# First token tiles on one DMA queue, the ScalarE table load ahead of its DMAs, and the up weights in a 3 + 4 split

## The chip, the core and the metric

The kernel runs on one core of a Trainium2 chip. The core has TensorE (matrix products, results in PSUM), VectorE (DVE), ScalarE (ACT), GpSimd (POOL) and SyncE (SP, which here only issues DMAs). DMAs are issued from the queues of SP and ScalarE and carried by 16 DMA engines. The metric is the device time of one execution in microseconds (us), the median of several runs; lower is better.

## The reference

The input x has 2048 tokens of width 448, in bf16. It is normalised per token (mean and variance, no scale), and the result goes into two branches whose outputs are added to x:

```
xn  = layernorm(x)
q, k, v = split(xn @ wqkv)            # 16 heads of 28
p   = softmax(q k^T * 28**-0.5)       # key j seen by query i if 0 <= i - j < 256
out = x + (p v) @ wo + (gelu(xn @ w_gate) * (xn @ w_up)) @ w_down     # inner width 1792
```

## The kernel before

Tokens are handled in 16 tiles of 128 and in four blocks of 512 queries. The program is written out in one order by hand. Each engine runs its own instructions in that order and waits on semaphores for the others, so an instruction that waits also holds up those behind it on its engine or queue.

**The start.** DMAs bring in the first token tiles (line 85: tile 0 on SP's queue; line 86: tile 1 on ScalarE's; line 87: tiles 2 and 3 on SP's). ScalarE then issues the first quarter of the query and of the key weights (line 89, into wraw), while SP issues the value weights (line 90), the weights of the last 64 input channels (lines 92 and 94), tiles 4 to 7 (line 95), the remaining query and key weights (line 97) and the up weights of five of seven pairs (line 98, through load_ffn, line 82, two DMAs, one for each half of the partitions). Each DMA takes the next of eight completion semaphores in turn, whichever queue it is issued from, and one that takes a semaphore a second time waits first for the earlier DMA to land. So SP can wait at line 97 for the DMAs that ScalarE issued at line 89.

Meanwhile DVE fills constants: eps, the zeros that TensorE's warm-up products read (line 124; the buffer is that of wo, whose weights arrive much later), the padding columns of the packed weights (lines 131 to 133), and masks, all ones at line 134, from which GpSimd later cuts triangles. At line 135 ScalarE loads the function table with ln and exp, which rstd needs.

TensorE runs nine warm-up products (line 150). For each of tiles 0 to 3 then follow: statistics on DVE (lines 155 and 156), the inverse deviation on ScalarE (160, 161), the normalisation on DVE (170), five transposes on TensorE (184, 186), and the copy of the transposed tile to xnT (187). A tenth warm-up product stands between the transposes of tiles 0 and 1. v_dense (line 191 through mm3) computes values, proj the first four heads' queries and keys, and qk_halves (197) adds the last 64 channels. DVE copies the keys to kT (245), and the scores (652), the exp (656) and the products with v (624) follow.

**Swapped copies.** The 448 input channels are 3.5 times 128. Work on 64-row halves runs two products side by side, one on each half of TensorE's rows, which needs x and some weights also with their halves exchanged. xsw is that copy of xnT, made by SP DMAs (swap, line 437); wvs (line 771) holds swapped value weights and wsq (line 443) swapped query and key weights. Tiles 4 and later are transposed by a DMA on SP's queue (line 176) instead of on TensorE.

**The first block.** In the plan of block 0 TensorE alternates between scores, the remaining projections and gen_up, which computes the up product of pairs of 128-column groups ahead of the gate (line 456, tiles ue). It does so for pairs 1, 2, 3, 0 and 4 in that order; for pairs 3 and 4 one of the two copies out of PSUM (line 473) is ScalarE's. Each pair reads its own columns of wu. Then come value, query and key products of the next block (lines 320 and 334), which read xsw, wvs and wsq, and then the gated part, which reads the gate weights wg and, for pairs 5 and 6, the rest of wu.

SP's order around the change: line 98's up weights, w3k (130), swap of block 0 (437), tiles 8 to 11 (740), the DMA transpose of tile 4 (176), wvs (771), the transposes of tiles 5 to 7, swap of block 1, wsq (443), the gate weights, the up weights of pairs 5 and 6 (line 788), tiles 12 to 15 (789), wo (793 and 794) and the down weights (797).

Of the kernel before, what the change touches and what calls it, by code (L numbers as in the profile page):

```python
# [13 lines left out]
f32 = mybir.dt.float32  # L14
i32 = mybir.dt.int32

S, D, H, Dh, F = 2048, 448, 16, 28, 1792
# [3 lines left out]
QB, NB = 512, 4  # L21
# [6 lines left out]
def kernel(  # L28
# [11 lines left out]
    nc = tc.nc  # L40
# [18 lines left out]
    xv = A_x.rearrange("b (n p) d -> p (b n) d", p=P)  # L59
# [3 lines left out]
    x_sb = const.tile([P, NT, D], bf16, name="x_sb")  # L63
# [4 lines left out]
    wu = const.tile([P, 7, F // 2], bf16, name="wu")  # L68
# [6 lines left out]
    def load_ffn(dst, w, pairs):  # L75

        wv64 = w.rearrange("(c p) (h n) -> p c h n", p=64, h=2)
        ns = slice(pairs.start * P, pairs.stop * P)  # L80
        for hi in range(2):
            nc.sync.dma_start(out=dst[64 * hi:64 * hi + 64, :, ns], in_=wv64[:, :, hi, ns])

    wqk = rows(A_wqkv, 0, 3)[:, :, 0:2 * D]
    nc.sync.dma_start(out=x_sb[:, 0, :], in_=xv[:, 0, :])
    nc.scalar.dma_start(out=x_sb[:, 1, :], in_=xv[:, 1, :])
    nc.sync.dma_start(out=x_sb[:, 2:4, :], in_=xv[:, 2:4, :])
    for c in (0, D):
        nc.scalar.dma_start(out=wraw[:, 0:3, c:c + 4 * Dh], in_=wqk[:, :, c:c + 4 * Dh])
    nc.sync.dma_start(out=wv[:, 0:3, :], in_=rows(A_wqkv, 0, 3)[:, :, 2 * D:3 * D])  # L90
# [4 lines left out]
    nc.sync.dma_start(out=x_sb[:, 4:8, :], in_=xv[:, 4:8, :])  # L95
    for c in (0, D):
        nc.sync.dma_start(out=wraw[:, 0:3, c + 4 * Dh:c + D], in_=wqk[:, :, c + 4 * Dh:c + D])
    load_ffn(wu, B_w_up, slice(0, 5))

    ident = const.tile([P, P], bf16, name="ident")  # L100
    make_identity(nc, ident[:, :])
# [6 lines left out]
    masks = const.tile([P, 3, 4, 64], bf16, name="masks")  # L108
# [11 lines left out]
    eps_t = const.tile([P, 1], f32, name="eps_t")  # L120
    nc.vector.memset(eps_t[:, :], 1e-5)
    warm = wo[:, :, :].rearrange("p g n -> p (g n)")
    for c in (slice(0, QB), slice(QB, 4 * D)):
        nc.vector.memset(warm[:, c], 0.0)
    wqp = const.tile([P, 3, H, 32], bf16, name="wqp")
    wkp = const.tile([P, 3, H, 32], bf16, name="wkp")
    w3p = const.tile([P, H, 32], bf16, name="w3p")
# [3 lines left out]
    nc.vector.memset(wqp[:, :, :, Dh:32], 0.0)  # L131
    nc.vector.memset(wkp[:, :, :, Dh:32], 0.0)
    nc.vector.memset(w3p[:, :, Dh:32], 0.0)
    nc.vector.memset(masks[:, :, :, :], 1.0)
    nc.scalar.preload_act_table_set("natural_log_exp_and_others")

    xnT = const.tile([P, 4, S], bf16, name="xnT")
    xsw = const.tile([P, 3, 2 * QB], bf16, name="xsw")
# [65 lines left out]
    def take(name, cols=QB, tag=None):  # L204

        tag = tag or spare[0]
        spare.remove(tag)  # L210
        ps = psum.tile([P, QB], f32, name=name, tag=tag, bufs=1)[:, 0:cols]
        held[id(ps)] = tag, ps
        return ps
# [46 lines left out]
    def gen_qk(gs, others):  # L260

        for g in gs:
            pq = take("pq")
            proj(pq, wqp, 0, g)
            yield 650
            pk = take("pk")
            proj(pk, wkp, 0, g)
            yield 650
            if g in others:
                v_half(*others[g])  # L270
            qk_halves(0, g, pq, pk)
            if g in others:
                v_copy(*others[g], nc.vector.tensor_copy)
            qk_copies(0, g, pq, pk)
            yield 360
# [187 lines left out]
    def gen_up(qb, ps, shared=()):  # L463

        for p in ps:
            us = [take("ue") for _ in range(2)]
            for c in range(7):
                chunk(us, wu, p, qb, c)
                if c < 6:
                    yield 213  # L470
            for i in range(2):
                copy = nc.scalar.copy if i and p in shared else nc.vector.tensor_copy
                copy(out=hTs[qb][:, p + 7 * i, :], in_=us[i])  # L473
            give(*us)
            yield 330
# [255 lines left out]
    pvs = [take("pv", D)]  # L731
# [6 lines left out]
    pads(nc.scalar.copy, wkp, slice(0, 1))  # L738
    swap(0)
    nc.sync.dma_start(out=x_sb[:, 8:12, :], in_=xv[:, 8:12, :])  # L740
    pvs.append(take("pv", D))
    v_dense(1, pvs[1])
    pvs.append(take("pv", D, "b2"))
# [34 lines left out]
    def ahead3():  # L778
        for t in (5, 6, 7):
            norm(t)  # L780
            dma_transp(t)
        swap(1, 4, 2)
        swap(1, 6, 2)
        fill_pads(False)
        swap_weights()
        load_ffn(wg, B_w_gate, slice(0, 3))
        load_ffn(wg, B_w_gate, slice(3, 7))
        load_ffn(wu, B_w_up, slice(5, 7))
        nc.sync.dma_start(out=x_sb[:, 12:16, :], in_=xv[:, 12:16, :])
        wo_v = A_wo.rearrange("(g j d) n -> j d g n", g=4, j=4)  # L790
        tail = A_wo[14 * Dh:, :].rearrange("(t i) n -> i t n", i=4)
        for j, (t0, n) in enumerate(SLOTS):
            nc.sync.dma_start(out=wo[32 * j:32 * j + Dh, 0:n, :], in_=wo_v[j][:, 0:n])
            nc.sync.dma_start(out=wo[32 * j + Dh:32 * j + 32, 0:n, :], in_=tail[:, t0:t0 + n])
        for k in range(0, NF, 4):
            n = min(4, NF - k)
            nc.sync.dma_start(out=wd[:, k:k + n, :], in_=rows(B_w_down, k, n))

    for qb in range(NB):
        if qb in (1, 3):  # L800
            tc.mark_branch_hint_location("general", hint="LikelyTaken",
                                         engines=[mybir.EngineType.DVE if qb == 1 else mybir.EngineType.PE])
        early = ()
        if qb == 0:
            new_hT(0)
            early = (0, 1, 2, 3, 4)
            u = chain(gen_qk((1, 2, 3), {1: (3, pvs[3]), 2: (2, pvs[2])}), gen_up(0, (1, 2, 3, 0, 4), (3, 4)))
            w = gen_pairs(1, (("v", 0), ("v", 2), ("k", 0), ("k", 1), ("k", 2)))
            plan = [[(u, 2), ahead, (u, 1)], [lambda: v_dense(2, pvs[2]), (u, 2), ahead2, (u, 1)],
                    [lambda: spare.append(spare.pop(1)), (u, 2), ahead3, (u, 4)], [lambda: stat(8), (u, 11)],  # L810
                    [lambda: stat(9), (u, 7), lambda: stat(10), (u, 7), lambda: fill_pads(True)], ["sums", (u, 7)],
                    ["inverse", "scale", (w, 11)], [(w, 10)],
                    [lambda: stat(11), (w, 7), lambda: rstd(8, 4), "sums", "inverse", (w, 7)]]
        else:
            d = gen_down(qb - 1)
            if qb < 3:
                u = gen_pairs(qb + 1, (("v", 0), ("k", 0), ("v", 2), ("k", 1), ("k", 2)))
                plan = [[(d, 14)], [(d, 11)], [(d, 11)], [(u, 7)], [(d, 18)], ["sums", (u, 7), "inverse"], [(u, 11)],
                        [lambda: q_last(qb + 1, nc.vector.tensor_copy), (d, 6), "sums"], [(d, 2), "inverse", (d, 10)],
                        [(u, 9), "masks", (u, 1)]]  # L820
                plan[3] = [(d, 1), (u, 7)]
                if qb == 2:
                    plan[0], plan[2] = [(d, 13)], [(d, 10)]
                if qb == 1:
                    for i, j in enumerate((0, 1, 2, 4)):
                        plan[j].insert(0, lambda t=12 + i: stat(t))
                    plan[4].append(lambda: rstd(12, 4))
                    plan[1] = plan[1][:1] + [lambda: q_last(1, nc.vector.tensor_copy), (d, 8)]
                    plan[2] = plan[2][:1] + [(d, 12), lambda: collect(1)]
                    plan[4].append(lambda: deliver(1))  # L830
            else:
                new_hT(3)
                early = (1, 2, 3, 4, 5, 6)
                u = gen_up(3, early, (4, 6))
                plan = [[(u, 12)], [(u, 9)], [(d, 12)], [(d, 10)], [(d, 12)], [(d, 1), (u, 7), "sums"], [(d, 12), "inverse"],
                        ["sums", "inverse", (d, 12)], [(d, 12)], [(u, 13), "masks", (u, 1)]]
        if qb in (1, 2):
            swap(qb + 1)
        score_pool(1)
        rest, after, flush = attention(qb, plan)  # L840
        nc.scalar.preload_act_table(ACT.Gelu_apprx_tanh)
        score_pool(2)
        if qb not in hTs:
            new_hT(qb)

        def hook(f):
            after(f)
            if qb in (1, 2) and f == 0:
                collect(qb + 1)
            if f == (8, 2, 2, 6)[qb]:  # L850
                o_collect(qb, nc.sync if qb else nc.scalar)
            if f == (12, 4, 4, 6)[qb]:
                o_deliver(qb)
                o_finish(qb)
            if qb == 0 and f == 6:
                nc.gpsimd.tensor_copy(out=wo[64:128, 3, :], in_=wo[0:64, 3, :])
            if qb in (1, 2) and f == 10:
                deliver(qb + 1)
            t = ({0: 8, 4: 9, 8: 10, 10: 11} if qb == 0 else {4: 12, 6: 13, 8: 14, 10: 15} if qb == 1 else {}).get(f)
            if t is not None:  # L860
                norm(t)
                dma_transp(t)

        gated(qb, early, rest, flush, hook)
        if qb < NB - 1:
            nc.scalar.preload_act_table_set("natural_log_exp_and_others")
# [156 lines left out]
```

## Time and profile before

| | |
|---|---|
| median of 3 runs | 214.47 us (214.2 to 214.63) |
| profiled execution, span from its first to its last instruction | 213.1 us |
| mean granted TensorE clock | 0.996 |
| TensorE busy | 207.6 us (97%) |
| DVE busy | 157.5 us (74%) |
| ScalarE busy | 131.6 us (62%) |
| GpSimd busy | 48.6 us (23%) |
| DMA traffic | 15.67 MB |

The profiled execution's own time is given by its span alone; the runs' times also hold what lies around the span, so that the median stands 1.4 us above it. In rows of the timeline the first number is the start, the second the length in microseconds, then the engine, the line, the operation and output<-inputs; xN means that N instructions are merged in the row. SPq and ACTq are the queues' issuing of DMAs, which is not the transfer itself; PEld is TensorE's loading of weights. A bracket at the end gives the idle time before the row and what ended it. A row of the chain of work is start, length and what. In rows by stretch of time the columns are the stretch, its length, then busy time (and count) of PE, PEld, DVE, ACT and POOL, the granted clock, the mean busy share of the DMA engines and GB/s. In a row of waits the last three numbers are the total in us, the count and the longest.

### The profile page before, as it was taken

How to read it: one execution, taken by the hardware profiler on the slowest of the kernel's cores; microseconds unless marked ns; L12 is line 12 of the kernel's file. 1: busy time of each engine (PE TensorE's matmuls, PEld its weight loads, DVE VectorE, ACT ScalarE, POOL GpSimd, SP SyncE). 2: the span in 40 equal slices, each digit the busy share in tenths (PEclk: the TensorE clock that was granted, in tenths of full speed). 3: DMA queues.
4: the chain of work that ended last, by engine and by line, in shares of the span. 5: the costliest groups of instructions: out<-in, count | busy, mean ns of one | idle time of the engine just before them, and what ended most of it. 6: DMA issues, size and time to landing. Idle time of an engine off the chain costs nothing.

```text
span 213.1 us, 6428 instructions
## 1 busy us (share of the span) xinstructions
PE 207.6 (97%) x2722; PEld 101.2 (47%) x2722; DVE 157.5 (74%) x355; ACT 131.6 (62%) x123; POOL 48.6 (23%) x86
## 2 busy tenths in 40 slices
PE   7999999999999999999999999999999999999992
PEld 2433444444454545444445445444445444544992
DVE  7899998999767985796536997495483898479531
ACT  4699578566777977423777887532676877665000
POOL 5287658451000220041000201022000022006001
PEclk9999999999999999999999999999999999999998
DMA  6999969979420101003421000001000101000011
GB/s 184 280 221 215 106 172 220 243 241 171 110 53 25 37 20 26 8 5 65 74 74 46 25 0 29 20 0 30 16 3 0 47 4 45 6 0 0 26 45 49
DMA packets 23993, 15.67 MB, mean 74 GB/s; under 512 B 9208, under 2 KB 23832, under 8 KB 23960
## 3 DMA queue, kind: packets, MB, share of 16 engines
q1 hardware_dynamic: 22918, 14.87, 31.2%
q8 instruction: 22, 0.36, 0.7%
q10 hardware_dynamic: 1042, 0.34, 0.7%
q14 instruction: 11, 0.09, 0.1%
HBM read 9.26 MB, written 2.41 MB: 55 GB/s over the span
## 4 chain that ended last, share of the span: by engine, by line
PE 94%; DVE 1%; ACT 1%; DMA 1%; issue 1%; DVEq 0%; ACTq 0%
PE po L393 26%; PE gt L456 20%; PE u L456 12%; PE ue L456 8%; PE pq L334 7%; PE sc L652 6%; PE ov L624 5%; PE pv L320 4%; PE pq L191 2%; PE pv L191 1%; DMA x_sb<-in_A_x_dram 1%; ACT p_sb L656 1%; DVE st L155 1%; PE s L191 1%; PE pk L191 1%
## 5 line engine op out<-in xcount | busy, mean ns | idle before, releaser
L656 ACT ACTIVATE p_sb<-sc 128x2048 bf16<-128x2048 f32 x39 | 73.2, 1878 | 20.5 <-PE sc L652 13.5
L496 ACT ACTIVATE p_sb<-gt 128x1024 bf16<-128x1024 f32 x28 | 28.7, 1025 | 33.6 <-PE gt L456 30.7
L591 POOL TENSOR_TENSOR oN<-oc,l 128x512 bf16<-128x512 f32 x16 | 21.5, 1355 | 120.0 <-DVE l L604 120.0
L393 PE MATMUL po<-wd,hT 128*128 128x448 bf16 (+1 forms) x266 | 46.2, 324 | 0.0
L456 PE MATMUL gt<-xnT,wg 64*128 64x512 bf16 x224 | 45.6, 376 | 0.0
L456 PE MATMUL gt<-xsw,wg 64*128 64x512 bf16 x168 | 40.7, 376 | 0.0
L504 DVE TENSOR_TENSOR hT<-p_sb,u 128x512 bf16<-128x512 bf16 x34 | 21.9, 677 | 16.0 <-PE u L456 15.8
L572 DVE TENSOR_TENSOR p_sb<-p_sb,masks 128x256 bf16<-128x256 bf16 (+1 forms) x90 | 27.8, 363 | 7.6 <-ACT p_sb L656 7.6
L393 PEld LDWEIGHTS <-hT 128*128 128x128 bf16 x266 | 24.5, 98 | 16.8 <-issue 2.2
L456 PEld LDWEIGHTS <-wg 64*128 64x128 bf16 x392 | 19.0, 94 | 22.5 <-issue 0.2
L456 PEld LDWEIGHTS <-wu 64*128 64x128 bf16 x392 | 18.7, 94 | 22.4 <-issue 0.8
L456 PE MATMUL u<-xnT,wu 64*128 64x512 bf16 x136 | 28.1, 376 | 0.0
L456 PE MATMUL u<-xsw,wu 64*128 64x512 bf16 x102 | 24.7, 376 | 0.0
L382 DVE TENSOR_TENSOR res<-po,x_sb 128x448 bf16<-128x448 f32 (+1 forms) x17 | 9.8, 592 | 11.6 <-PE po L393 9.3
L456 PE MATMUL ue<-xnT,wu 64*128 64x512 bf16 x88 | 18.0, 377 | 0.0
L652 PE MATMUL sc<-qT,kT 28*64 28x320 bf16 (+7 forms) x648 | 16.4, 261 | 0.1
L456 PE MATMUL ue<-xsw,wu 64*128 64x512 bf16 x66 | 16.4, 377 | 0.0
L582 POOL TENSOR_SCALAR_AFFINE_SELECT p_sb<-p_sb 128x512 bf16<-128x512 bf16 (+1 forms) x21 | 14.2, 702 | 6.6 <-ACT p_sb L656 6.5
L609 DVE TENSOR_TENSOR oc<-oc,ov 128x512 f32<-128x512 f32 x12 | 8.2, 681 | 8.7 <-ACT oc L608 8.7
L652 PEld LDWEIGHTS <-kT 28*64 28x64 bf16 (+1 forms) x648 | 7.5, 102 | 13.3 <-issue 12.0
L393 PE MATMUL po<-wo,oN 128*128 128x448 bf16 (+1 forms) x70 | 13.0, 320 | 0.0
L473 DVE CAST hT<-ue 128x512 bf16<-128x512 f32 x18 | 11.6, 679 | 1.9 <-PE ue L456 1.8
(108 smaller groups left out, 276.9 us busy)
## 6 DMA issues: line engine op xcount, KB each, us to landing
out_dram<-res SPq DMA_DIRECT2D x15, 112.0 KB
x_sb<-in_A_x_dram SPq DMA_DIRECT2D x3, 448.0 KB
wd<-in_B_w_down_dram SPq DMA_DIRECT2D x3, 448.0 KB
xsw<-xnT SPq DMA_DIRECT2D x6, 192.0 KB
wu<-in_B_w_up_dram SPq DMA_DIRECT2D x2, 560.0 KB
wg<-in_B_w_gate_dram SPq DMA_DIRECT2D x2, 448.0 KB
wg<-in_B_w_gate_dram SPq DMA_DIRECT2D x2, 336.0 KB
wraw<-in_A_wqkv_dram SPq DMA_DIRECT2D x2, 252.0 KB
```

The lines of the kernel that those rows point to most:

```text
L334: nc.tensor.matmul(ps, lhsT=w.rearrange("p h d -> p (h d)"), rhs=xchunk(qb, hi, c, qb * QB, QB), start=c == 0, stop=c == 6, tile_position= ...
L393: nc.tensor.matmul(po[:, a:b], lhsT=x[:, k, tt * P:(tt + 1) * P], rhs=wt[:, k, lo + a:lo + b], start=start and n == a == 0, stop=stop and ...
L456: nc.tensor.matmul(ps, lhsT=w[64 * hi:64 * hi + 64, c, p * P:(p + 1) * P], rhs=xchunk(qb, hi, c, qb * QB, QB), start=c == 0, stop=c == 6, ...
L473: copy(out=hTs[qb][:, p + 7 * i, :], in_=us[i])
L496: nc.scalar.activation(out=ges[p][:, :, :], in_=gt[:, :, :], func=ACT.Gelu_apprx_tanh)
L504: nc.vector.tensor_tensor(out=hT[:, p + 7 * i, :], in0=ge[:, i, :], in1=u, op=ALU.mult)
L572: nc.vector.tensor_tensor(out=reg, in0=reg, in1=m, op=ALU.mult)
L582: nc.gpsimd.affine_select(out=reg, in_=reg, pattern=mid + [[1 if diag else -1, min(w, P)]], compare_op=ALU.is_ge, fill=0.0, base=0 if diag ...
L591: nc.gpsimd.tensor_tensor(out=oN[:, g, :], in0=oc[:, :], in1=inv, op=ALU.mult)
L624: nc.tensor.matmul(ov[half or 0][32 * j:32 * j + 32, q0:q0 + nq], lhsT=v_sb[r, kt, 4 * g + j, :], rhs=p_sb[r, j, col:col + nq], start=n == ...
L652: nc.tensor.matmul(ss[k0:k0 + nk, j, col:col + nq], lhsT=kT[r, g, kt * P + k0:kt * P + k0 + nk], rhs=qT[r, g, ring(qb).start + q0:ring(qb) ...
L656: nc.scalar.activation(out=p_sb[:, :, 0:ncol], in_=ss[:, :, 0:ncol], func=ACT.Exp, scale=SCALE)
```

## The change

Tile 1 moves to SP's queue, between tile 0 and tiles 2 and 3. ScalarE loads its table before it issues the two weight DMAs. The up weights come in the parts 0 to 2 and 3 to 6 instead of 0 to 4 and 5 to 6, and the second part stands behind tiles 8 to 11, ahead of the DMA transposes. The ahead-of-gate order of pairs becomes 1, 2, 0, 3, 4, with ScalarE sharing the copies of pairs 0 and 4. The zeros beyond the 512 columns that the warm-up reads are no longer written. masks is set through a view of 32-bit words, half as many, each of them two bf16 ones (the bits 3F803F80).

```
     nc.sync.dma_start(out=x_sb[:, 0, :], in_=xv[:, 0, :])
-    nc.scalar.dma_start(out=x_sb[:, 1, :], in_=xv[:, 1, :])
+    nc.sync.dma_start(out=x_sb[:, 1, :], in_=xv[:, 1, :])
     nc.sync.dma_start(out=x_sb[:, 2:4, :], in_=xv[:, 2:4, :])
+    nc.scalar.preload_act_table_set("natural_log_exp_and_others")
     for c in (0, D):
         nc.scalar.dma_start(out=wraw[:, 0:3, c:c + 4 * Dh], in_=wqk[:, :, c:c + 4 * Dh])
...
-    load_ffn(wu, B_w_up, slice(0, 5))
+    load_ffn(wu, B_w_up, slice(0, 3))
...
-    for c in (slice(0, QB), slice(QB, 4 * D)):
-        nc.vector.memset(warm[:, c], 0.0)
+    nc.vector.memset(warm[:, 0:QB], 0.0)
...
-    nc.vector.memset(masks[:, :, :, :], 1.0)
-    nc.scalar.preload_act_table_set("natural_log_exp_and_others")
+    nc.vector.memset(masks[:, :, :, :].rearrange("p a b c -> p (a b c)").bitcast(f32), 1 + 0x3F80 / 2**23)
...
     nc.sync.dma_start(out=x_sb[:, 8:12, :], in_=xv[:, 8:12, :])
+    load_ffn(wu, B_w_up, slice(3, 7))
...
         load_ffn(wg, B_w_gate, slice(3, 7))
-        load_ffn(wu, B_w_up, slice(5, 7))
...
-            u = chain(gen_qk(...), gen_up(0, (1, 2, 3, 0, 4), (3, 4)))
+            u = chain(gen_qk(...), gen_up(0, (1, 2, 0, 3, 4), (0, 4)))
```

More of the change, by code (lines that the diff above doesn't have):

```diff
@@ L806 @@
             early = (0, 1, 2, 3, 4)
-            u = chain(gen_qk((1, 2, 3), {1: (3, pvs[3]), 2: (2, pvs[2])}), gen_up(0, (1, 2, 3, 0, 4), (3, 4)))
+            u = chain(gen_qk((1, 2, 3), {1: (3, pvs[3]), 2: (2, pvs[2])}), gen_up(0, (1, 2, 0, 3, 4), (0, 4)))
             w = gen_pairs(1, (("v", 0), ("v", 2), ("k", 0), ("k", 1), ("k", 2)))
```

## The prediction

> **What bounds the kernel now.** I read the page first, then the chain of work that ended last in order of time, then the timeline of the first 33 us, because every edit lies there. The page:
>
> ```profile
> span 213.1 us, 6428 instructions
> PE 207.6 (97%) x2722; PEld 101.2 (47%) x2722; DVE 157.5 (74%) x355; ACT 131.6 (62%) x123; POOL 48.6 (23%) x86
> PE 94%; DVE 1%; ACT 1%; DMA 1%; issue 1%; DVEq 0%; ACTq 0%
> ```
>
> TensorE is 94% of the chain, and no matmul is added or taken away. So the change can win only where TensorE waits, and 213.1 less 207.6 leaves 5.5 us of that in all. The chain's first pieces (start, length, what) show where:
>
> ```profile
> 0.82 2.45 DMA x_sb<-in_A_x_dram
> 3.29 0.64 DVE st L155
> ...
> 6.46 0.48 ACT xnT L187
> ...
> 6.99 0.74 PE pv L191 x3
> ...
> 11.71 0.38 PE sc L652 x8
> ...
> 12.16 1.89 ACT p_sb L656
> ```
>
> The first token tile lands at 0.82 + 2.45 = 3.27, the statistics, the normalisation and the copy of the transposed tile follow, and TensorE's first useful product (v_dense of tile 0, line 191) begins at 6.99. From there the chain is TensorE, but for one exp (12.16). Before 6.99 the chain is a DMA and DVE: that is what the edits at the top of the kernel touch. The same stretch as a timeline (start, length, engine, line):
>
> ```profile
> 0.82 0.39 SPq L85 DMA_DIRECT2D x_sb<-in_A_x_dram  x1
> 0.82 0.42 ACTq L86 DMA_DIRECT2D x_sb<-in_A_x_dram  x1
> 1.27 0.42 SPq L87 DMA_DIRECT2D x_sb<-in_A_x_dram  x1
> 1.27 1.01 ACTq L89 DMA_DIRECT2D wraw<-in_A_wqkv_dram  x2
> 1.39 4.02 PE L150 MATMUL wps<-wo 128*128 128x512 bf16 x9 [1.39 <-DVE wo L124]
> 2.31 1.28 ACT L135 ACT_TABLE_LOAD   x1 [2.31 <-issue]
> 2.37 0.70 DVE L134 MEMSET masks<- 128x768 bf16 x1
> 4.17 0.29 ACT L160 ACTIVATE lnv<-mv_all,eps_t 128x1 f32<-128x1 f32 x1 [0.58 <-DVE mv_all L156]
> 4.77 0.59 SPq L95 DMA_DIRECT2D x_sb<-in_A_x_dram  x1
> 5.20 0.53 PE L184 MATMUL tp<-ident,xn 128*128 128x128 bf16 x3
> 6.64 0.11 PEld L186 LDWEIGHTS <-xn 128*64 128x64 bf16 x2
> 7.84 0.27 DVE L711 COPY wqp<-wraw 128x336 bf16<-128x336 bf16 x1
> 8.28 0.11 PEld L186 LDWEIGHTS <-xn 128*64 128x64 bf16 x2
> 8.46 0.30 PEld L191 LDWEIGHTS <-xnT 128*128 128x128 bf16 x3
> 9.10 0.62 DVE L155 BATCH_NORM_STATS2 st<-x_sb 128x6 f32<-128x448 bf16 x1
> 10.49 0.18 DVE L156 BATCH_NORM_AGGREGATE mv_all<-st 128x2 f32<-128x6 f32 x1
> 10.91 0.69 DVE L245 CAST kT<-s 128x512 bf16<-128x512 f32 x1 [0.24 <-PE s L197]
> 11.57 0.62 SPq L740 DMA_DIRECT2D x_sb<-in_A_x_dram  x1
> 13.62 1.32 SPq L176 DMA_TRANSPOSE xnT<-xn  x1
> ```
>
> **The change, part by part.** *DVE's memsets.* The second memset of wo goes and masks shrinks from 768 halfwords to 384 words. The group row prices the first:
>
> ```profile
> L124 DVE MEMSET wo<- 128x640 uint32 x1 | 0.6, 592 | 0.1
> ```
>
> 384 words at 592/640 ns each are 0.36 us, so DVE is free 0.59 + 0.34 = 0.93 us sooner, at 3.07 - 0.93 = 2.14. Worth nothing alone: the statistics began at 3.29 because of the DMA's 3.27. It is a condition for the next term: without it DVE would be busy to 3.07 and cap that gain at 0.2.
>
> *The first tiles on one queue.* Tile 0 no longer starts beside tile 1 from ScalarE's queue; tile 1 is issued one step later, at 1.27 (the step from line 85 to 87 is 0.45 us). The row of the DMA engines while both moved (core 0, half a microsecond; the last column is GB/s):
>
> ```profile
> 2.50:3.00 0.50, 0.50 (x2) 0.15 (x1) 0.50 (x1) 0.50 (x1) 0.50 (x2) 1.00 0.98 290
> ```
>
> Tile 1's 112 KB at 290 GB/s are 0.39 us. Tile 0 gains between 0 (its 2.45 us are latency) and 0.39; interleaved packet by packet it would lose most of that to tile 1 now, but 128 KB of small weight packets still share the engines, so I take 0.25. It cannot lose, since nothing is put ahead of it. Tile 1 is wanted one statistic and its aggregate (0.64 + 0.18) after tile 0's new 3.02, at about 3.8, and one issue step behind tile 0 lands at about 3.5: hidden. Tiles 2 and 3, a further step behind, land at about 4.3 with twice the size, against 4.7 for the third statistic: hidden too. [...]
>
> *What TensorE makes of 0.25 us.* Not all. The nine warm-up products run from 1.39 and the first transpose follows them at 5.20 back to back, so that start is fixed by TensorE, as is the second tile's transpose, whose last weight load is at 6.64. From such a load to the next product's took 8.46 - 8.28 = 0.18 in the later pair. So v_dense can begin at 6.64 + 0.18 = 6.82 at the earliest: 6.99 - 6.82 = 0.17 is the cap. ScalarE's copy, 0.25 sooner, ends at 6.69 and does not bind. Taken: 0.15.
>
> *One more issue on SP.* Every DMA behind tile 1 on SP is issued 0.45 later, tiles 4 to 7 at 5.22 instead of 4.77. Statistic 4 reads them at 9.10, with DVE not waiting. If that data came just then, it comes at 9.55, the two statistics end 0.45 later at 11.12, and the key copy, which now has 0.24 of slack (10.91 against 10.67), is 0.21 late instead of 0.15 early. If the data came early it costs nothing. From the issue, 2.45 us (tile 0's) and the other 336 KB at 290 GB/s, 1.2 us, make 8.4 now and 8.9 after: before 9.10 - 0.15 = 8.95, barely. Taken 0; the range keeps 0.36.
>
> *ScalarE's queue.* The table load goes from 2.31 to about 0.85 and ends at about 2.1; its first user came at 4.17, so it costs nothing. The two weight DMAs are then issued at 0.85 if issuing runs past the load, at 2.1 if it waits: 0.4 earlier or 0.85 later than 1.27. DVE reads the first at 7.84, not waiting. But SP waits for the second:
>
> ```profile
> SPq L97 <- DMA wraw<-in_A_wqkv_dram: 0.9, 1, 0.9
> SPq L771 <- DMA wu<-in_B_w_up_dram: 1.3, 1, 1.3
> ```
>
> So SP's queue from there moves between 0.9 earlier and 0.85 later. Its transfers were backed up then (next row), so I take 0.
>
> *Up weights in two parts.* Two pairs, 448 KB, leave the place ahead of swapped x; at the rate of that stretch they are 2.0 us:
>
> ```profile
> 12.00:14.00 2.00, 1.97 (x13) 0.69 (x10) 1.80 (x7) 1.84 (x2) 1.71 (x7) 1.00 1.12 227
> 22.00:23.00 1.00, 1.00 (x26) 0.39 (x20) 1.00 (x3) 0.00 (x0) 1.00 (x2) 1.00 0.25 26
> 24.00:25.00 1.00, 1.00 (x12) 0.49 (x10) 0.97 (x3) 1.00 (x1) 0.00 (x0) 1.00 0.02 5
> 29.00:30.00 1.00, 1.00 (x20) 0.49 (x18) 1.00 (x3) 0.80 (x2) 1.00 (x1) 1.00 0.21 49
> ```
>
> Swapped x was in time for its first product even so (18.86 below, with no wait). Their two new issues fit on SP between 12.2 (11.57 + 0.62) and 13.62, where it waited for DVE's normalised tile 4. Behind x tiles 8 to 11 now stand four pairs, 896 KB, 4.0 us at 227 GB/s, so the DMA transposes of tiles 4 to 7, the swapped value weights, the next swapped x and the swapped query and key weights stand 4.0 - 2.0 = 2.0 us further back. But the engines were 75% idle from 22 to 23 and 98% from 24 to 25, which takes up 1.7 of the 2.0. What is left, 0.3, meets these rows:
>
> ```profile
> 18.86 0.59 PE L456 MATMUL ue<-xsw,wu 64*128 64x512 bf16 x2
> ...
> 27.05 0.55 SPq L443 DMA_DIRECT2D wsq<-wkp  x1
> ...
> 29.37 0.53 PE L320 MATMUL pv<-wvs,xsw 64*128 64x448 bf16 x2
> ...
> 32.27 0.28 PEld L334 LDWEIGHTS <-wsq 64*128 64x128 bf16 x2
> ```
>
> The swapped weights, issued at 27.05, were through by about 30 (share 0.21 from 29 to 30) or 31 at the latest, and are read at 32.27: slack 1.3 to 2.3. So 0.3 costs nothing; the full 2.0 would cost up to 2.0 + 0.15 - 1.3 = 0.85. I take 0 and keep 0.85. Gelu's gate weights stand behind these and are read only after 37 us. The pair that now comes fourth, 3, needs the second part after about 25 us; that part is through by about 22 (16.9, where SP's wait for the up weights ended, less 2.0, plus swapped x, tiles 8 to 11 and 4.0). Pair 0 in third place lies in the first part. The last two pairs' DMA further down disappears, which gives the 2.0 us back before the down weights.
>
> *Sum.* -0.15 with every other term hidden: 213.1 becomes 212.95. The median of the runs is 214.47, 1.4 above the profiled span, and I leave that distance as it is: 214.3.
>
> **Rivals.** *Faster by over 0.2% (0.43 us, about what a measurement of this kernel can tell from no change).* TensorE takes 4.02 us for nine warm-up products against 0.74 for three later ones (448 columns against 512), with a granted clock of 1.00 in the rows by stretch: its rate rises during the front. If in most executions it rises sooner than here, the cap of 0.17 is gone, tile 0's full 0.39 passes through, and with a little of SP's earlier queue the time is 214.0. [...] Chance 0.22.
>
> *No gain.* Tile 0's 2.45 us is latency, or statistic 4 waits for tiles 4 to 7 and the key copy gives the 0.15 back: 214.5. For it: 8.9 against 8.95 above. Against: DVE's slack of 0.24. Chance 0.20.
>
> *Slower.* The four pairs ahead of the transposes make the swapped query and key weights late and TensorE, in order, stands at 32.27. It decides once they are more than 1.3 us later, and at the full 2.0 the time is 214.47 - 0.15 + 0.85 = 215.2. For it: SP issues the next swapped x only after the transposes have landed, so idle DMA time there may be waiting and not room. Against: the idle 1.7. Chance 0.18.
>
> **How the numbers follow.** Forecast 0.40, no gain 0.20, faster 0.22, slower 0.18. The forecast and no gain both lie within 0.43 of 214.47, so same is 0.60. The range takes the faster case's 214.0 with 0.2 for its spread, 213.8, and the slower case to half its price, 214.9; the forecast's own range is 214.1 to 214.5.
>
> **What would show it.** Right: the chain's first DMA shorter by about 0.25, the first line 191 product at 6.8, exp at about 12.0, the swapped weights' load at about 32.1 with no wait for a DMA. Wrong: DVE waiting for tile 4's statistic, ScalarE's weight DMAs holding SP past 7 us, or a TensorE gap before line 320 or 334 with the transposes' DMA behind it. A step at 6.99 that does not move says that tile 0 gained nothing.

## The result, and the profile after

The changed kernel takes 216.33 us (median; 215.19 to 218.0) against 214.58 (214.2 to 215.04) for the kernel before, a ratio of 1.0084 with a 95% interval of 1.0065 to 1.0104. It is slower by 0.84%. The forecast was 214.3 in a range of 213.8 to 214.9, so both the size and the sign are wrong. The profiled execution took 216.46 us with a span of 214.7, against a span of 213.1 before. Lines from the memsets on carry numbers lower by one than before (line 190 is v_dense, 319 the value products of the next block, 436 swapped x).

The page of the changed kernel, head and chain:

```profile
span 214.7 us, 6423 instructions
...
PE 207.7 (97%) x2718; PEld 101.2 (47%) x2722; DVE 156.7 (73%) x354; ACT 131.6 (61%) x123; POOL 48.6 (23%) x86
...
PE 87%; DMA 7%; DVE 1%; ACT 1%; issue 1%; SPq 1%; DVEq 0%; ACTq 0%
```

TensorE is as busy as before (207.7 against 207.6 us), so the 1.6 us are waits. DMA went from 1% of the chain to 7%. The chain of waits in order of time, to the last of its DMAs, and TensorE's waits up to 60 us:

```profile
1.74 4.28 DMA x_sb<-in_A_x_dram
...
7.25 0.20 ACT rstd_all L160
7.45 0.48 ACT xnT L186
...
7.98 0.74 PE pv L190 x3
...
19.66 6.97 DMA xnT<-xn
...
26.65 0.62 SPq L436
...
27.32 4.09 DMA xsw<-xnT
```

```profile
PE tp L183 <- DVE xn L169: 0.8, 1, 0.8
PE pv L319 <- DMA xsw<-xnT: 0.8, 1, 0.8
```

The first DMA of the chain is no longer tile 0's at 0.82 but that of tiles 2 and 3, issued at 1.74 and landed at 6.02. Two DMA pieces that were not on the chain before follow it: the transposes of tiles 5 to 7, and a part of swapped x that lands at 31.41. The timeline of the changed kernel, SP and ScalarE issuing, DVE's statistics and TensorE's consumers; the last row is of the kernel before, the third statistic:

```profile
0.82 1.28 ACT L88 ACT_TABLE_LOAD   x1 [0.82 <-PEq L1006]
0.85 0.99 ACTq L90 DMA_DIRECT2D wraw<-in_A_wqkv_dram  x2
...
1.61 0.38 DVE L134 MEMSET masks<- 128x384 f32 x1
1.74 0.43 SPq L87 DMA_DIRECT2D x_sb<-in_A_x_dram  x1
...
3.04 0.63 DVE L154 BATCH_NORM_STATS2 st<-x_sb 128x6 f32<-128x448 bf16 x1 [1.05 <-DMA x_sb<-in_A_x_dram]
...
6.04 0.37 SPq L96 DMA_DIRECT2D x_sb<-in_A_x_dram  x1
6.04 0.63 DVE L154 BATCH_NORM_STATS2 st<-x_sb 128x6 f32<-128x448 bf16 x1 [1.15 <-DMA x_sb<-in_A_x_dram]
...
7.23 0.34 PE L183 MATMUL tp<-ident,xn 128*128 128x128 bf16 x3 [0.76 <-DVE xn L169]
...
7.98 0.74 PE L190 MATMUL pv<-wv,xnT 128*128 128x448 bf16 x3 [0.23 <-ACT xnT L186]
...
31.46 0.36 PE L319 MATMUL pv<-wvs,xsw 64*128 64x448 bf16 x2 [0.76 <-DMA xsw<-xnT]
...
210.73 0.55 PE L392 MATMUL po<-wo,oN 128*128 128x224 bf16 x4
```

```profile
5.06 0.62 DVE L155 BATCH_NORM_STATS2 st<-x_sb 128x6 f32<-128x448 bf16 x1
```

Three readings. Tile 0 did gain its quarter of a microsecond: its statistic starts at 3.04, not at 3.29. But the third statistic waits until 6.04, not 5.06, for tiles 2 and 3, and v_dense of tile 0 begins at 7.98 instead of 6.99: **+0.99**. (ScalarE copies tile 0 only after the third tile's deviation: the chain's pieces at 7.25 and 7.45.) Then the first product with swapped x begins at 31.46 instead of 29.37, +2.09 in all: **another +1.10** there, 0.76 of it a wait, the rest the product with xnT (0.36 at 30.34) that before ran side by side with it (29.36 and 29.37) and here ran alone ahead of the wait. Nothing further is lost up to the last products, which began at 208.63 before:

```profile
208.63 0.55 PE L393 MATMUL po<-wo,oN 128*128 128x224 bf16 x4
```

That is +2.10 there against +1.6 in the span. The tail behind the last products was 0.5 shorter in this execution; why stays open.

The DMA engines over the two places, before and then after (rows by stretch, GB/s last):

```profile
3.00:3.50 0.50, 0.50 (x3) 0.15 (x2) 0.27 (x2) 0.50 (x1) 0.50 (x1) 1.00 1.03 321
3.50:4.00 0.50, 0.50 (x3) 0.23 (x2) 0.47 (x2) 0.10 (x1) 0.17 (x1) 1.00 1.18 285
```

```profile
3.00:3.50 0.50, 0.50 (x3) 0.16 (x2) 0.46 (x1) 0.00 (x0) 0.50 (x1) 1.00 0.98 187
3.50:4.00 0.50, 0.50 (x3) 0.22 (x2) 0.47 (x3) 0.08 (x1) 0.16 (x1) 1.00 0.66 155
...
27.00:28.00 1.00, 1.00 (x16) 0.27 (x14) 0.90 (x3) 0.03 (x1) 0.94 (x5) 1.00 0.04 9
...
30.00:31.00 1.00, 0.70 (x13) 0.21 (x9) 1.00 (x3) 0.80 (x2) 1.00 (x1) 1.00 0.06 9
```

Between 3 and 4 us the engines moved little more than half the bytes they moved before (171 GB/s against 303 in the mean), with ScalarE's weights among them, whose rows are of 224 bytes (four heads of 28 in bf16; a token's row has 896). Packets under 512 bytes, nearly all of these weights, number 456 from 2 to 3 us, where before it was 32. From 30 to 31, just where TensorE waits, their share is 0.06, that is one engine of sixteen.

### The profile page after: what moved, and what is told of

Same layout as the page of the kernel before. It is cut to its first block, busy times and chain, and to the rows that moved or that the text cites. A ratio compares the mean times of both kernels' runs of the same rounds, so it can differ in the third digit from the quotient of the medians.

```text
span 214.7 us, 6423 instructions
## 1 busy us (share of the span) xinstructions
PE 207.7 (97%) x2718; PEld 101.2 (47%) x2722; DVE 156.7 (73%) x354; ACT 131.6 (61%) x123; POOL 48.6 (23%) x86
## 4 chain that ended last, share of the span: by engine, by line
PE 87%; DMA 7%; DVE 1%; ACT 1%; issue 1%; SPq 1%; DVEq 0%; ACTq 0%
PE po L392 26%; PE gt L455 20%; PE u L455 12%; PE pq L333 6%; PE sc L651 6%; PE ue L455 4%; PE ov L623 4%; PE pv L319 4%; DMA xnT<-xn 3%; DMA x_sb<-in_A_x_dram 2%; DMA xsw<-xnT 2%; PE pv L190 1%; PE pq L190 1%; ACT p_sb L655 1%; PE s L190 1%
## 5 line engine op out<-in xcount | busy, mean ns | idle before, releaser
L651 PE MATMUL sc<-qT,kT 28*64 28x320 bf16 (+7 forms) x648 | 16.4, 262 | 0.1
L455 PE MATMUL ue<-xsw,wu 64*128 64x512 bf16 x66 | 16.4, 378 | 0.0
```

The costliest lines, as they stand in the source:

```text
L455: nc.tensor.matmul(ps, lhsT=w[64 * hi:64 * hi + 64, c, p * P:(p + 1) * P], rhs=xchunk(qb, hi, c, qb * QB, QB), start=c == 0, stop=c == 6, ...
L651: nc.tensor.matmul(ss[k0:k0 + nk, j, col:col + nq], lhsT=kT[r, g, kt * P + k0:kt * P + k0 + nk], rhs=qT[r, g, ring(qb).start + q0:ring(qb) ...
```

## The experiments

Theory: two losses, both of the order in which bytes reach the DMA engines. **First**, ScalarE's weight DMAs, freed from tile 1, start 0.42 us earlier (0.85 for 1.27), while tiles 2 and 3 start 0.47 later (1.74 for 1.27), so that those weights now move beside tiles 2 and 3. **Second**, the 448 KB of up weights put ahead of the transposes make swapped x late. Rivals: the later issue of tiles 2 and 3 alone; the order of the pairs; the memsets or the table load; an instruction fetch among the parts of swapped x (the last section).

**The memsets alone.** Kernel before with

```
-    for c in (slice(0, QB), slice(QB, 4 * D)):
-        nc.vector.memset(warm[:, c], 0.0)
+    nc.vector.memset(warm[:, 0:QB], 0.0)
-    nc.vector.memset(masks[:, :, :, :], 1.0)
+    nc.vector.memset(masks[...].rearrange(...).bitcast(f32), 1 + 0x3F80 / 2**23)
```

> The kernel before with DVE's shorter memsets alone (512 zeros, masks as 32-bit words). Every theory: within 0.3 us of before, 214.5 to 215.0, and DVE idle before the first statistic. A rival worth its own look: if the bits of masks or the missing zeros mattered to the time at all, it would show here and nowhere else.

Measured: 214.81 us, ratio 0.9998 (0.9982 to 1.0015). The memsets do nothing.

**The start's edits alone** (memsets, tile 1 on SP, table load first; up weights as before):

```
-    nc.scalar.dma_start(out=x_sb[:, 1, :], in_=xv[:, 1, :])
+    nc.sync.dma_start(out=x_sb[:, 1, :], in_=xv[:, 1, :])
     nc.sync.dma_start(out=x_sb[:, 2:4, :], in_=xv[:, 2:4, :])
+    nc.scalar.preload_act_table_set("natural_log_exp_and_others")
```

> The kernel before with the edits of the start alone: tile 1 on SP's queue, the table load ahead of ScalarE's DMAs, the shorter memsets; the up weights stay 5 + 2 in the old order. Theory A (tiles 2 and 3, now a step later on SP, land late and hold up the third tile's statistic, 0.99 us in the changed kernel's trace): slower than before by 0.5 to 1.2 us, 215.1 to 215.8, scattered by over 1 us from run to run as the changed kernel is, with DVE waiting for x_sb at the third statistic. Rival (the late landing was one DMA engine's chance stall, which any kernel can meet, and the whole loss is that of the up weights): 214.3 to 214.7, scattered by under 1 us.

Measured: 216.84, ratio 1.0076 (1.0047 to 1.0105), above what the theory gave. The wait for tiles 2 and 3 is there again (0.77 at the third statistic, which starts at 5.82), and no wait at 30 us. But the loss grows after the wait. This kernel's rows by stretch (the sixth number is the granted clock):

```profile
5.80:7.50 1.70, 0.65 (x6) 0.28 (x5) 1.63 (x4) 0.77 (x3) 0.00 (x0) 1.00 0.80 201
7.50:9.20 1.70, 1.47 (x8) 0.69 (x6) 1.04 (x4) 1.18 (x4) 0.00 (x0) 0.50 1.03 336
9.20:10.90 1.70, 1.70 (x11) 0.78 (x10) 0.55 (x3) 0.96 (x2) 0.00 (x0) 0.50 1.11 306
10.90:12.60 1.70, 1.70 (x10) 0.66 (x10) 1.48 (x6) 0.50 (x2) 1.35 (x7) 0.99 1.05 220
```

TensorE was busy 0.65 of 1.70 us, and its granted clock then stood at 0.50 for 3.4 us (three value products in 1.30 us at 7.76; before they took 0.74). v_dense began at 7.76 (+0.77); the products with swapped x at 31.45 (+2.08). So the wait costs itself and, in this execution, 1.3 us more of slow products. Of its five runs three have a mean clock of 0.992 and took 216.84 to 217.2; the two at 1.0 took 215.75 and 215.88. The changed kernel has two of nine at 0.992 (216.81 and 218.0). What sets the length of the slow stretch, 7.5 to 10.9 us in these rows, is not shown.

**The up weights alone.** Kernel before with

```
-    load_ffn(wu, B_w_up, slice(0, 5))
+    load_ffn(wu, B_w_up, slice(0, 3))
...
     nc.sync.dma_start(out=x_sb[:, 8:12, :], in_=xv[:, 8:12, :])
+    load_ffn(wu, B_w_up, slice(3, 7))
...
-        load_ffn(wu, B_w_up, slice(5, 7))
...
-            ... gen_up(0, (1, 2, 3, 0, 4), (3, 4)))
+            ... gen_up(0, (1, 2, 0, 3, 4), (0, 4)))
```

> The kernel before with the up weights' 3 + 4 split and the new order of pairs alone; the start is as before. Theory B (896 KB ahead of the DMA transposes make the next swapped x late at line 320, 1.1 us in the changed kernel's trace): slower by 0.7 to 1.3 us, 215.3 to 215.9, with a gap on TensorE between 29 and 31 us and the third tile's statistic at about 5.1 as before. Rival (the late swapped x was itself a consequence of the late start): within 0.3 us of before, no gap.

Measured: 215.82 (214.93 to 216.86), ratio 1.0044 (1.0022 to 1.0065). The profiled execution was the shortest of its runs, with no gap at swapped x (29.39) and a loss of only 0.28 at the swapped weights (32.55 for 32.27). Two further profiled executions:

> The split of the up weights alone, 3 + 4, looked at again, because its first profile was of its fastest run. Theory (swapped x comes too late in the typical execution): a run near 215.8 has a gap of 0.3 to 1.5 us before line 319 with swapped x behind it, or a load of swapped query and key weights that waits. Rival: the loss lies elsewhere, spread over the span or in its tail, and line 319 begins at about 29.4 again.

> The same kernel, a third execution; expected as of the second.

Measured: 215.03 and 214.43, beside 215.2 (214.66 to 215.56) for the kernel before in that comparison; these two executions show no loss. In the three profiles swapped x is issued at 25.44, 25.24 and 25.06; before it was 23.68. The timeline of SP, first of the kernel before, then of the second of the three with the load of the swapped weights:

```profile
18.67 4.54 SPq L176 DMA_TRANSPOSE xnT<-xn  x3
23.68 2.62 SPq L437 DMA_DIRECT2D xsw<-xnT  x4
```

```profile
18.71 3.83 SPq L176 DMA_TRANSPOSE xnT<-xn  x3
25.24 2.62 SPq L437 DMA_DIRECT2D xsw<-xnT  x4
...
32.80 0.10 PEld L334 LDWEIGHTS <-wsq 64*128 64x128 bf16 x2 [0.41 <-DMA wsq<-wkp]
```

The transposes are issued at the same time, but SP can go on to swapped x only when they have landed, 1.4 to 1.8 us later than before. What shows is a wait of 0.17 and 0.41 us for the swapped weights in the first two, and none for a DMA in the third; the products with swapped x (29.39 to 29.42) do not wait. No profile is of a typical run of 215.8, so where most of this kernel's own loss goes stays open.

**Half of those bytes.** Three parts on the kernel before, with the pair order of the change (the first part again 0 to 2; only the added lines are shown):

```
+    load_ffn(wu, B_w_up, slice(3, 6))      # behind tiles 8 to 11
...
+        load_ffn(wu, B_w_up, slice(6, 7))  # behind the gate weights
```

> The kernel before with the up weights in three parts, 3 + 3 + 1, and the pair order of the change: 224 KB more ahead of the transposes instead of 448. Theory (idle DMA time behind the transposes is waiting, so each 448 KB move swapped x by nearly 4 us against 2.8 us of slack): half of it moves it by about 2, it lands at about 28.5, before its read at 29.4; the time is 214.7 to 215.3, between the kernel before and the full split. Rival (the order of the pairs costs, not the bytes): 215.8 as with the full split.

Measured: 215.24, ratio 1.0033 (1.0016 to 1.005), inside what the theory gave, with swapped x issued at 24.05, and no wait for a DMA at lines 320 and 334 in the trace. The theory had the move of swapped x wrong: 0.37 us later (24.05 for 23.68), not about 2. The profiled execution was again the shortest, and where the 0.33% goes is not shown. The medians stand in the order of the bytes, though the interval overlaps that of the full split.

**The changed kernel with the last two pairs back behind the gate weights** (3 + 2 + 2):

```
-    load_ffn(wu, B_w_up, slice(3, 7))
+    load_ffn(wu, B_w_up, slice(3, 5))
...
         load_ffn(wg, B_w_gate, slice(3, 7))
+        load_ffn(wu, B_w_up, slice(5, 7))
```

> The changed kernel with the up weights in three parts, 3 + 2 + 2: pairs 3 and 4 behind tiles 8 to 11, pairs 5 and 6 where they were before, so that as many bytes stand ahead of the DMA transposes as before. Theory B: the gap at the value products of the next block is gone and 1.0 to 1.2 us come back, 215.1 to 215.4, what is left being the start's. Rival (the gap came from the late start or from the 16 KB instruction fetch, not from the bytes): still 216 to 216.5 with the gap.

Measured: 217.41, ratio 1.0148 (1.0079 to 1.0216); its four runs took 216.14, 216.21, 218.61 and 219.2. In the profiled one (216.21) v_dense starts at 7.82 (+0.83) and the first product with swapped x at 30.20 (+0.83):

```profile
30.20 0.53 PE L319 MATMUL pv<-wvs,xsw 64*128 64x448 bf16 x2
```

The second loss is gone, as expected, the first is there. The median was not expected. A further profiled execution:

> The changed kernel with the up weights in 3 + 2 + 2 parts, looked at again, because two of its four runs took about 219 us and none of those was profiled. Theory: a longer wait for tiles 2 and 3, or a granted clock at half for 3.4 us after that wait, at 7 to 11 us; no gap before line 319. Rival: a loss in a place that no profile has shown yet.

Measured: 218.64 in the profiled execution and 216.18 in the other. The rows by stretch and groups of that execution, with the transposes ahead of v_dense, and those of the kernel before from the same point of the program on:

```profile
7.05 0.50 PE L183 MATMUL tp<-ident,xn 128*128 128x128 bf16 x3 [0.53 <-DVE xn L169]
```

```profile
7.90:14.00 6.10, 6.10 (x22) 2.26 (x22) 2.74 (x10) 2.31 (x7) 2.51 (x11) 1.00 1.09 272
```

```profile
L190 PE MATMUL s<-xnT,wqp 128*128 128x512 bf16 x3 | 1.5, 634 | 0.0
```

```profile
7.00:13.10 6.10, 6.10 (x43) 2.50 (x43) 5.01 (x17) 4.35 (x10) 3.30 (x14) 1.00 1.05 276
```

```profile
L191 PE MATMUL s<-xnT,wqp 128*128 128x512 bf16 x3 | 0.8, 382 | 0.0
```

In 6.1 us TensorE finished 22 products instead of 43, with 634 ns for one instead of 382, and no wait. So this long run has the first loss again (v_dense began at 7.80, +0.81) and a slow rate until about 14 us, which cost 2.8 more (in the chain line 319's products begin at 32.99, where before they began at 29.42: +3.57). The slow rate did not begin with the wait: the transposes take 0.50 at 7.05 as they took 0.53 at 5.20, where in the changed kernel they are back to 0.34 at 7.23. In this execution the rate of the start lasted on, over and past the wait. The other long runs were not profiled. The granted clock's column shows 1.00 there; the length of the products tells it, the column does not.

**The changed kernel with tile 1 back on ScalarE's queue:**

```
-    nc.sync.dma_start(out=x_sb[:, 1, :], in_=xv[:, 1, :])
+    nc.scalar.dma_start(out=x_sb[:, 1, :], in_=xv[:, 1, :])
```

> The changed kernel with tile 1 back on ScalarE's queue, ahead of the table load, so that tiles 2 and 3 are issued at 1.27 again; all else as changed. Theory A: the third statistic starts near 5 us without a wait, 0.7 to 1.2 us come back, 215.2 to 215.6, and the scatter falls; the gap at the value products stays. Rival (chance stall): no change, 216 to 216.5.

Measured: 216.13 (215.93 to 217.64), ratio 1.0064 (1.0048 to 1.0081). The time is where the rival had it, but the trace is not: the first loss is gone, as the third statistic starts at 5.04 with no wait, v_dense at 6.97. The profiled execution was the longest, and its chain names other DMAs:

```profile
7.01 6.62 DMA wraw<-in_A_wqkv_dram
14.57 1.51 DVE xn L169 x2
20.33 7.45 DMA xnT<-xn
28.46 3.83 DMA xsw<-xnT
32.34 2.25 PE pv L319 x21
```

The rest of the query and key weights landed at 13.63, and swapped x later still, +2.97 at its first product. One late transfer in the first 14 us makes the second loss larger: in the chain two of DVE's normalisations follow these weights, at 14.57, and the transposes, issued at 20.33 instead of 18.67, need the normalised tiles.

**Both moves of bytes undone** (the last two edits together; memsets, table load and pair order as changed):

> The changed kernel with both of its moves of bytes undone: tile 1 on ScalarE's queue ahead of the table load and the up weights in 3 + 2 + 2, so that as many bytes as before stand ahead of the DMA transposes. Theory B (the 448 KB more ahead of the transposes are the second loss, about 1 us in the median): within 0.3 us of before, 214.5 to 215.1, no gap at line 319 or 333. Rival (the third part, or the place of the parts, does it and not the bytes): stays near the split alone, 215.8.

Measured: 214.85, ratio 1.0014 (1.0000 to 1.0028); v_dense at 7.01, first product with swapped x at 29.39. Both losses are gone, which also clears the table load and the pair order, to within the interval. The losses do not add: the start's edits alone have 1.0076, the up weights alone 1.0044, the changed kernel 1.0084.

**The weight DMAs later.** The changed kernel, and the kernel with the start's edits alone, with ScalarE's two weight DMAs after its first inverse deviation (rstd):

```
-    for c in (0, D):
-        nc.scalar.dma_start(out=wraw[:, 0:3, c:c + 4 * Dh], in_=...)
...
     rstd(0, 1)
+    for c in (0, D):
+        nc.scalar.dma_start(out=wraw[:, 0:3, c:c + 4 * Dh], in_=...)
```

> The changed kernel with ScalarE's two weight DMAs issued after the first inverse deviation, at about 4.3 us instead of 0.85; tile 1 stays on SP. Theory A1 (the small weight packets, moved 0.42 us forward when tile 1 left ScalarE's queue, run beside tiles 2 and 3 and hold them up): tiles 2 and 3 land by 4.4, the third statistic starts near 4.9 without a wait, about 0.8 us come back, 215.2 to 215.8 with the second loss left. Theory A2 (the later issue on SP alone makes them late): they still land near 6 and nothing comes back, 216 to 216.6. A third way: the late weights hold SP's remaining weight DMAs and their users at 7.5 to 8.5, and the loss moves there.

> The start's edits alone, with the up weights as before, and ScalarE's two weight DMAs issued after the first inverse deviation. Theory A1: the start's loss is gone and what the prediction expected is left, 214.4 to 214.8, first line 187 to 191 product at about 6.8. Theory A2: as the start alone, 215.7 to 217. If the time is right and the clock falls back to half in none of the runs, the clock was a consequence of the wait.

Measured: 216.32, ratio 1.0065 (1.0041 to 1.0089), and 215.19, ratio 1.0018 (0.9998 to 1.0038). The first is where theory A2 had it, the second between the two, so the times do not decide; the traces do. With the weights issued at 4.14 and 4.04, the third statistic starts at 4.70 and 4.78, not at 6.04:

```profile
4.70 0.62 DVE L152 BATCH_NORM_STATS2 st<-x_sb 128x6 f32<-128x448 bf16 x1
```

Tiles 2 and 3, still issued at 1.74, are in time. So it was the weights beside them, not the later issue. And no run of the two kernels has a mean clock below 0.996, where 0.992 appears with the start's edits alone. In the first of these v_dense starts at 6.89, 0.10 sooner than before, the only place where the gain of the start is seen. It is lost at tiles 4 to 7, which the weights now meet (the second profile is of its longest run, 216.18). The fifth statistic of the two kernels (at 9.10 and not waiting before):

```profile
10.03 0.63 DVE L152 BATCH_NORM_STATS2 st<-x_sb 128x6 f32<-128x448 bf16 x1 [0.66 <-DMA x_sb<-in_A_x_dram]
```

```profile
10.82 0.63 DVE L152 BATCH_NORM_STATS2 st<-x_sb 128x6 f32<-128x448 bf16 x1 [1.63 <-DMA x_sb<-in_A_x_dram]
```

**The weight DMAs on SP's queue behind tiles 2 and 3**, in the changed kernel and with 3 + 2 + 2:

```
-        nc.scalar.dma_start(out=wraw[:, 0:3, c:c + 4 * Dh], in_=...)
+        nc.sync.dma_start(out=wraw[:, 0:3, c:c + 4 * Dh], in_=...)
```

> The changed kernel, with the two DMAs of the first query and key weights on SP's queue behind tiles 2 and 3 instead of on ScalarE's. Theory (these weights are moved beside tiles 2 and 3 and hold them up): behind them in one queue they cannot, so tiles 2 and 3 land by about 4.6, DVE's third statistic waits under 0.3 us and v_dense of tile 0 begins at 6.8 to 7.1; tiles 4 to 7 are issued about 0.9 us later, which may cost 0.3 to 1.0 at the fifth statistic, and the gap before line 319 stays, so the median is 215.2 to 216.2. Rival (the later issue alone, 0.47 us behind, makes tiles 2 and 3 late): they land at 5.8 or later as in the changed kernel and v_dense begins at about 8.0.

> The same with the up weights in three parts, 3 + 2 + 2, so that both moves of bytes are mended while tile 1 stays on SP's queue. Theory (two losses, both of order on the DMA engines): no wait of DVE for tiles 2 and 3, no gap before line 319, 214.3 to 214.9, or up to 215.4 if tiles 4 to 7 now come late. Rival (tile 1 on SP's queue costs by itself): over 215.5.

Measured: 216.65, ratio 1.0102 (1.008 to 1.0123), and 216.31, ratio 1.0074 (1.0053 to 1.0095). The third statistic starts at 4.75 and 5.03 with no wait, as the theory said. Its price was wrong: both medians lie above what I gave, and the second (216.31) where the rival, that tile 1 on SP costs by itself, had it. But with tile 1 on SP and the weights later the start came to 215.19; here something else is late. TensorE's waits of the two kernels:

```profile
PE pv L319 <- DMA xsw<-xnT: 0.8, 1, 0.8
PE pv L190 <- DMA wv<-in_A_wqkv_dram: 0.5, 1, 0.5
```

```profile
PE pv L190 <- DMA wv<-in_A_wqkv_dram: 1.1, 1, 1.1
```

Now the value weights are late, since they stand behind the query and key weights in one queue. (In the second, tile 1 was also 0.27 late for its statistic.) In the second kernel that wait too is followed by a granted clock of 0.50 (9.2 to 10.9 us), and the loss is +2.2 by 11.25 (first product with the query weights, 9.05 before). By its wait alone (v_dense at 7.86, +0.87) it would have come out near 215.5; in the profiled execution, the longest of its four, the slow rate took the rest.

**Over the profiles.** The third statistic starts at 5.82 to 6.04 in the four with the weights beside tiles 2 and 3, at 4.70 to 5.03 in the four with tile 1 on SP too but the weights later, and at 5.04 to 5.06 in three with tile 1 on ScalarE's queue (the kernel before, the changed kernel with tile 1 back, both moves undone). From SP's issue of the transposes of tiles 5 to 7 to its issue of swapped x, or in the chain to their landing, pass 5.01 us in the kernel before and 4.87 with both moves undone, 5.41 in the one with 224 KB more ahead, and 6.34 to 7.45 in the seven with 448 KB more.

No kernel tried beats the kernel before. The start holds at most 0.17 us by the prediction's cap, and each order of the first transfers that takes it makes tiles 2 and 3, the value weights or tiles 4 to 7 late.

## Why the prediction was wrong

- **DVE's memsets**: right. They end at 1.99, before the first statistic, and alone change nothing.
- **The first tiles on one queue**: the 0.25 for tile 0 was right in this execution (3.29 to 3.04; 3.12 to 3.19 in the three others with the weights beside), though the weights that share the engines are two DMAs of 84 KB, not 128 KB in all. With them out of the way tile 0's statistic starts at 2.83 to 2.98, about the full 0.39. The sentence "Tiles 2 and 3, a further step behind, land at about 4.3 ... hidden too" is the step that failed first. It took their issue step and size, and a rate from a row in which other things moved. It did not ask what would start sooner. They landed at 6.02. "It cannot lose, since nothing is put ahead of it" holds for tile 0, not for the tiles behind it: nothing is put ahead of them on SP but tile 1, yet the weights now move beside them.
- **ScalarE's queue**: "0.4 earlier" was right to the number (0.85 for 1.27), and the table load was free. But only SP's later wait for these weights was weighed. What they share the engines with in those 0.4 us was not. From 2 to 3 us ScalarE's queue (q10 in the DMA view) moved 433 packets beside 220 of SP's (q1), where before it was 143 beside 164. How an engine chooses between two queues is not shown; what it cost is: with the weights behind tiles 2 and 3 in one queue, or issued at 4.1, the third statistic starts at 4.7 to 5.0, and at 5.8 to 6.0 with them beside.
- **What TensorE makes of 0.25 us**: the cap of 0.17 was not contradicted; 0.10 is the most that a trace showed. What the step left out is the other direction: a late tile costs its wait, and in some executions the rate afterwards.
- **One more issue on SP**: thin, as it said ("8.9 against 8.95"). In the changed kernel SP issues tiles 4 to 7 at 6.04, because that DMA waits for tiles 2 and 3 to land (0.8 us in SP's waits). With the weights at 4.1 it was the fifth statistic that waited, 0.66 and 1.63 us.
- **Up weights in two parts**: the second failed step. Of the 2.0 us, 1.7 were said to be taken up by idle engines. The idle time was SP's waiting: swapped x is issued only when the transposes have landed (SP's longest wait for them at that line is 2.4 us before, 2.8 after), and the idle row from 24 to 25 even lies behind its issue at 23.68. Alone the split moved that issue by 1.4 to 1.8 us, nearly the 2.0 and not 0.3; in the changed kernel by 2.97 (23.68 to 26.65), of which 0.99 are the transposes' later issue (19.66 for 18.67), the first loss passed on, and 1.98 their later landing. The slack was taken from the swapped weights' read at 32.27, and that is where the split alone waited; in the changed kernel the one that went was that of swapped x at 29.37.
- **The rivals**: "Slower" had the mechanism ("may be waiting and not room") and, for the split alone, the place; in the changed kernel the wait came earlier, at swapped x. It had half the loss: its 0.85 is near the 0.9 us of the split alone (0.44% of 214.8), but no trace shows that time lost where the rival had it, so the nearness may be luck. The 0.99 of the start stands in no rival. "Faster" asked for a rate that rises sooner: it had by 5.2 us in two of the profiles (transposes of 0.34 at 5.11 and 5.17 instead of 0.53 at 5.20), and in both a wait followed and the rate fell back. The list of what would show it wrong did name the gap before line 319 (320 then), and it is there.

For the profiled execution the sum should have read +0.99 at the start and +1.1 at swapped x, where it had -0.15 and 0.

## What to carry to other kernels

When an edit takes a DMA off one queue, work out what starts sooner on that queue, and what it then moves beside, not only what the moved DMA gains. Idle time on the DMA engines was no room here for a transfer that was not yet issued (98% idle from 24 to 25 us, and swapped x issued 1.4 to 1.8 us later all the same); look at what the issuing queue waits for before counting it. A wait of TensorE near the start cost more than its length in one execution of the start's edits alone (0.77 us at v_dense was 2.08 at the products with swapped x), and small gains there are to be set against slack that single late transfers use up.

## What was not expected of the hardware

A wait of TensorE of 0.53 to 1.14 us between 6 and 8 us was followed by a granted clock of 0.50 in some executions and not in others. In two whose products had been fast before the wait (the transposes 0.34 at 5.11 and 5.17) the granted clock fell to 0.50 afterwards, for 3.4 us in the start's edits alone. In the long execution of 3 + 2 + 2 the products had been slow before it and stayed so until 14 us (22 products for 43), with a granted clock of 1.00 in the column. In the profiled run of the change they became fast across the wait (0.53 at 5.20, 0.34 at 7.23) and stayed so. No run moved the wait against the rise of the rate, so what decides it is not shown.

An instruction fetch of 0.02 MB falls near the swapped copies. The DMA view, before from 27.4 to 28 us, and after from 28 to 29:

```profile
q8 instruction: 1, 0.02, 16.4%
```

```profile
q8 instruction: 1, 0.02, 9.8%
```

16.4% of sixteen engines for 0.6 us, or 9.8% for 1 us, are both 1.57 us of one engine, counted whole where the packet starts. Before, it fell behind swapped x (issued from 23.68); after, swapped x is issued from 26.65 and the fetch falls among its parts, the second of which took 4.09 us to land while one engine in sixteen was at work (the row from 30 to 31). That the fetch is what held that engine is read from the coincidence; no run moved it. In the second profile of the split alone a fetch also fell among them (0.02 MB, 12.3% from 27.5 to 28.2, swapped x issued from 25.24 to 27.86), and swapped x was in time. So how much of the 0.76 us of wait at swapped x is the fetch's, and how much that of the 2.97 us later issue, stays open.
